# Block 6 of the first expert layer moves from direct products to seven block products per pair of tiles, in a three-layer fp32 kernel on one core

## The chip, the cores and the metric

The kernel runs on one NeuronCore of one Trainium2 chip. The metric is the device time of one execution in microseconds (us), smaller is better. Engines are named as in the profile: PE is TensorE (PEld its weight loads), DVE is VectorE, ACT is ScalarE, POOL is GpSimd, SP is SyncE, whose queue (SPq) issues all the transfers here.

## The reference

```
q_s = softmax(q, over head_dim);  k_s = softmax(k, over seq)          # 8 x 8 x 576 x 64
attn = q_s @ (k_s^T @ v)           ->  x: 4608 tokens x 512
h = x @ w_in (512 x 2048);  g = elu(h);  x = g @ w_out                # layer 1
h = x @ w2_in;  g = P(h) / Q(h), a cubic over a quadratic in |h|;  out = g @ w2_out   # layer 2
```

All of it is float32. The inputs are scaled by 8, so full precision matters.

## The kernel before, in words

**Precision.** A float32 matrix product is made of three fp32r products: each operand is split into a high and a low part (`copy_hi`, `sub_lo`), and high·high, high·low and low·high are summed in PSUM.

**Blocks and tiles.** The 4608 tokens are nine blocks of 512 (`NB` = 9, `j` = 0 to 8), the 2048 hidden columns sixteen tiles of 128 (`KF` = 16, `f`). A step is one tile of one block, in the order of the list `tiles`.

**Direct form** (layer 1, blocks 0 to 6): `plan_in` (L1157) makes a tile of h by 12 products of 128x512 into a PSUM bank (L1169 to L1171); ACT and DVE form elu and its two parts (`plan_elu`, L1372); `plan_out` (L1191) adds 12 products of 128x512 into the accumulators (L1208). A pair of tiles is 24 products in and 24 out.

**Seven-product form** (layer 1, blocks 7 and 8, and all of layer 2): `plan_group` (L1471) makes two tiles as a 2x2 block product by seven products of sums (m1 to m7 at L1559 on). Each is six matmuls of 128x256 (L1508), 42 in all, into a pair of PSUM banks; between them ACT copies two quarters (u1, u5, L1517) and DVE adds two (d2, d1, L1522), and m6, m7 and m4 wait for those. The out half is the same 24 matmuls of 128x512 (L1601 in layer 1, L1741 in layer 2). The sums of weights (`w1f` for layer 1, `wf` for layer 2) and of x (`x0`, `x1`) are formed beforehand by DVE, POOL and ACT, saved to DRAM and loaded again: every group loads 1.75 MB of weight sums (`plan_ring`, L1421, loads named `ring`), and every block seven forms of x (`plan_xf`, loads named `xf`).

`J0` is the first block in this form; there are `N1` = (9 - J0) * 8 groups in layer 1. The eight weight sums of layer 1 are formed once (`plan_w1f`), whatever J0 is.

**Attention.** Pairs of heads: load k and v, softmax of k over the sequence, the key-value product (`kv_pair`, L774, issued by `plan_unit`, L1063), the softmax of q (`plan_q`), and x itself (`x_mm` in `plan_x`, L887). `at_step` and `x_step` say at which step a pair's key-value product and x are wanted; the tables `EARLIER` and `X_STEP` override them. In layer 1's groups x is computed in a pair of banks between two groups (`in_pair`, `between`), and the forms of x go straight to their tiles (`plan_here`); for block J0 alone they go through DRAM (`x0_d`).

**The order.** A planner (`Plan`) sets it when the program is built: every operation has engines, a cost, what it waits for and a rank; `run` picks the next one by the earliest start and then the rank, and the engines get their instructions in that order. `NUDGE` adds to the rank of single operations by number, `W2FROM` and `W2STEP` say at which steps layer 2's weights are converted (32 loads `st`, `plan_w2`). Each engine, and the SP queue, then runs its list in order.

```
for p in range(HALF if J0 < NB else 0):
    plan_w1f(p, W1FROM + W1STEP * p)
...
for j in range(J0, NB):
    plan_xf(0, j)
    for p in range(HALF):
        plan_group(0, j, p)
```

Of the kernel before, what the change touches and what calls it, by code (L numbers as in the profile page):

```python
# [25 lines left out]
J0 = 7  # L26
# [21 lines left out]
W2FROM, W2STEP = 44, 2.4  # L48
# [27 lines left out]
NUDGE = {3: 12, 20: -40.7, 27: 71.1, 37: 14.9, 45: 23.6, 47: -20.6, 57: -10.7, 58: -13.2, 60: 28.4, 68: -37, 69: -15.2, 70: -43.5, 94: -35.9, 95: 27, 99: 8.1, 104: 3, 109: -5.8, 112: 4.2, 121: 19.8, 130: 52.7, 131: -5.5, 135: 33.7, 158: 18.9, 168: 27.2, 209: 8.6, 211: 28.6, 213: 1.2, 221: 4.8, 223: -3.4, 226: 66.8, 235: 75.5, 250: 40.1, 278: 66.9, 304: -20.3, 313: 0.7, 315: -48.8, 650: 18.7, 656: 6.8, 694: 35.3, 908: 6.8, 918: 28.6, 1619: -25.7, 1624: 17.2, 1756: 11.5, 1822: 3.2, 1839: -3.7, 1884: 15.7, 1890: 5.2, 1892: 18.7, 1909: -1.9, 1953: -8.3, 1978: 17.9, 2019: -6.8, 2029: -11.1, 2205: 18.9, 2433: -5.3, 2911: 59.4, 2946: 10, 2964: 31.4, 2994: 9.7, 3002: -4.3}  # L76
# [210 lines left out]
def linear_attention_elu_rational(  # L287
# [295 lines left out]
    def plan_w2(f, which, rank, after):  # L583
# [23 lines left out]
        b["op"] = op(SP, load, after, rank - 1, take=[kinds], extra=6.0, move=MB)  # L607
        o, x = plan_f32(b["op"], lambda: b["st"], high, DM, rank, [], front)
        if which:
# [1326 lines left out]
```

## Time and profile before

| | |
|---|---|
| median of 3 runs | 1531.74 us (1531.17 to 1534.08) |
| the profiled execution: time, span | 1529.98 us, 1528.2 us |
| PE busy | 1517.4 us, 99% of the span |
| PEld, DVE, ACT, POOL busy | 89%, 77%, 69%, 37% |
| granted TensorE clock | 1.0 (2.4 GHz) in all slices |
| DMA | 358.90 MB, 235 GB/s over the span |

The span runs from the first to the last instruction; the time is 1.78 us longer. The busy share of PE counts a matmul to its modelled end, so two matmuls overlap in it: what one costs is read from the distance of starts. In the slices PE stands at 9 tenths or more in all but the first and the last.

### The profile page before, as it was taken

Reading aid. Unit: us, or ns where it says so; the run is one execution under the profiler, and the core shown is the slowest. Engines: PE = TensorE matmul, PEld = TensorE weight load, DVE = VectorE, ACT = ScalarE, POOL = GpSimd, SP = SyncE. Lnnn points to the kernel's source line nnn. Section 1 sums busy time; section 2 is a strip of 40 time slices with the busy share of each in tenths; the row PEclk is TensorE's granted clock in tenths of the full one; section 3 lists DMA queues with packets and bytes.
Section 4 is the critical chain, followed back from the end, with each engine's and each line's share of the span. In section 5 each row is a group of like instructions: output and inputs, shape, how many; then the busy total and the mean of one; then the engine's idle time right before and its main releaser. Section 6 shows DMA issues by size and latency. Waiting matters only on the chain.

```text
span 1528.2 us, 26062 instructions
## 1 busy us (share of the span) xinstructions
PE 1517.4 (99%) x9916; PEld 1361.5 (89%) x9916; DVE 1171.7 (77%) x1710; ACT 1061.8 (69%) x1630; POOL 572.9 (37%) x355
## 2 busy tenths in 40 slices
PE   8999999999999999999999999999999999999998
PEld 6888888888888888898999999999999999999998
DVE  8998899776869888577656787777777777777776
ACT  7877666665757666576557777777777777777775
POOL 3103344221313222033125775444444444444442
PEclk9999999999999999999999999999999999999999
DMA  9622775444544555787999987766767675757561
GB/s 372 260 84 74 239 269 198 167 174 149 195 153 160 183 197 221 257 291 288 335 370 387 371 286 259 255 255 227 270 212 274 218 280 207 290 206 275 207 228 49
DMA packets 99997, 358.90 MB, mean 235 GB/s; under 512 B 9760, under 2 KB 22048, under 8 KB 85536
## 3 DMA queue, kind: packets, MB, share of 16 engines
q1 hardware_dynamic: 99872, 357.23, 64.5%
q8 instruction: 78, 1.28, 0.3%
q14 instruction: 47, 0.39, 0.1%
HBM read 271.21 MB, written 85.98 MB: 234 GB/s over the span
## 4 chain that ended last, share of the span: by engine, by line
PE 96%; DVE 2%; DMA 1%; issue 0%; ACT 0%; POOL 0%; SPq 0%; DVEq 0%; POOLq 0%
PE pair L1508 26%; PE acc L1741 24%; PE acc L1208 19%; PE ps L1169 6%; PE ps L1171 6%; PE ps L1170 6%; PE acc L1601 5%; PE ps L784 1%; PE ps L916 1%; DMA st<-in_moe_w_in_dram 0%; DMA e<-in_q_dram 0%; PE ps L796 0%; DVE mx L845 0%; DVE bits L459 0%; DVE mx L815 0%
## 5 line engine op out<-in xcount | busy, mean ns | idle before, releaser
L1508 PEld LDWEIGHTS pair<-xf,ring 128*128 128x128 f32 x3696 | 453.4, 192 | 16.6 <-ACT pair L1517 1.3
L1508 PE MATMUL pair<-xf,ring 128*128 128x256 f32 x3696 | 456.1, 275 | 1.2 <-ACT pair L1517 0.9
L1741 PE MATMUL acc<-w_out,g 128*128 128x512 f32 x1728 | 407.4, 379 | 0.0
L1741 PEld LDWEIGHTS acc<-w_out,g 128*128 128x128 f32 x1728 | 311.1, 190 | 35.1
L1208 PE MATMUL acc<-gs,w_out 128*128 128x512 f32 x1344 | 310.5, 380 | 0.0
L1643 POOL TENSOR_TENSOR s<-s,a 128x1024 f32<-128x1024 f32 x72 | 170.6, 2369 | 338.8 <-ACT s L1635 316.7
L1208 PEld LDWEIGHTS acc<-gs,w_out 128*128 128x128 f32 x1344 | 252.5, 189 | 38.1 <-issue 1.0
L1169 PE MATMUL ps<-xp,w_in 128*128 128x512 f32 x448 | 171.6, 383 | 0.0
L1522 DVE TENSOR_TENSOR pair<-pair,u 128x256 f32<-128x256 f32 x176 | 75.9, 431 | 122.9 <-PE pair L1508 122.7
L1170 PE MATMUL ps<-xp,w_in 128*128 128x512 f32 x448 | 169.8, 379 | 0.0
L1171 PE MATMUL ps<-xp,w_in 128*128 128x512 f32 x448 | 169.8, 379 | 0.0
L438 POOL TENSOR_TENSOR g<-p,g 128x1024 fp32r<-128x1024 f32 x70 | 166.9, 2384 | 7.7 <-POOL s L1643 0.4
L1630 ACT ACTIVATE a<-pair,b_sb 128x1024 f32<-128x1024 f32 (+1 forms) x73 | 80.4, 1103 | 125.6 <-PE pair L1508 125.6
L1660 DVE TENSOR_TENSOR p<-p,pair 128x1024 f32<-128x1024 f32 (+1 forms) x73 | 88.1, 1206 | 71.9 <-ACT s L1635 67.3
L435 ACT ACTIVATE gs<-halves 128x512 fp32r<-128x512 f32 x112 | 70.5, 630 | 73.7 <-DVE halves L1396 33.6
L1390 ACT ACTIVATE halves<-ps 128x512 f32<-128x512 f32 x112 | 66.4, 593 | 58.0 <-PE ps L1171 56.8
L1396 DVE SCALAR_TENSOR_TENSOR halves<-halves,ps 128x512 f32<-128x512 f32 x112 | 75.7, 678 | 34.9 <-ACT halves L1393 34.5
L1169 PEld LDWEIGHTS ps<-xp,w_in 128*128 128x128 f32 x448 | 84.6, 189 | 15.1 <-issue 2.4
L1656 DVE SCALAR_TENSOR_TENSOR a<-s,a 128x1024 f32<-128x1024 f32 (+1 forms) x73 | 95.7, 1312 | 2.4
L1171 PEld LDWEIGHTS ps<-xp,w_in 128*128 128x128 f32 x448 | 84.7, 189 | 12.0
L1667 DVE SCALAR_TENSOR_TENSOR p<-p,a_sb,a 128x1024 f32<-128x1024 f32 (+1 forms) x74 | 93.5, 1265 | 2.5
L1170 PEld LDWEIGHTS ps<-xp,w_in 128*128 128x128 f32 x448 | 84.7, 189 | 11.5
(178 smaller groups left out, 2258.9 us busy)
## 6 DMA issues: line engine op xcount, KB each, us to landing
ring<-wf SPq DMA_DIRECT2D x72, 1024.0 KB, 5.1
ring<-wf SPq DMA_DIRECT2D x72, 768.0 KB, 7.1
x<-fo SPq DMA_DIRECT2D x60, 512.0 KB, 3.2
xf<-x SPq DMA_DIRECT2D x30, 1024.0 KB, 7.8
ring<-w1f SPq DMA_DIRECT2D x16, 1024.0 KB, 5.4
wf<-fo SPq DMA_DIRECT2D x24, 512.0 KB, 3.1
ring<-w1f SPq DMA_DIRECT2D x16, 768.0 KB, 7.2
out_dram<-e SPq DMA_DIRECT2D x36, 256.0 KB, 2.2
```

Of the source, the lines that this page charges most:

```text
L438: engine[e].tensor_tensor(out=lo, in0=src, in1=hi.bitcast(F32), op=ALU.subtract)
L1169: nc.tensor.matmul(o, w[:, 0, kk, :], two(x[:, 0]), start=(kk == 0), stop=False)
L1170: nc.tensor.matmul(o, w[:, 0, kk, :], two(x[:, 1]), start=False, stop=False)
L1171: nc.tensor.matmul(o, w[:, 1, kk, :], two(x[:, 0]), start=False, stop=(kk == KD - 1))
L1208: nc.tensor.matmul(turned(o), lhsT, two(rhs), start=(f == f0 and n == 0), stop=(f == f1 and n == 2))
L1508: apart(nc.tensor.matmul(o, lhsT, two(rhs), start=start and n == 0, stop=n == 5, skip_group_check=True), "PE", where[region])
L1630: nc.scalar.activation(out=b["a"][:, c], in_=h(), func=AF.Abs, scale=b_sb[:, 0:1])
L1643: engine[e].tensor_tensor(out=b["s"][:, c], in0=b["s"][:, c], in1=b["a"][:, c], op=ALU.add)
L1656: nc.vector.scalar_tensor_tensor(out=b["a"][:, c], in0=b["s"][:, c], scalar=-2.0, in1=b["a"][:, c], op0=ALU.add, op1=ALU.mult)
L1660: nc.vector.tensor_tensor(out=b["p"][:, c], in0=b["p"][:, c], in1=h(), op=ALU.mult)
L1667: nc.vector.scalar_tensor_tensor(out=b["p"][:, c], in0=b["p"][:, c], scalar=a_sb[:, 0:1], in1=b["a"][:, c], op0=ALU.add, op1=ALU.mult)
L1741: nc.tensor.matmul(turned(o), b["g"][:, gl, c], two(wo[:, wl_]), start=p == 0 and q == 0 and n == 0, stop=p == KF // 2 - 1 and q == 1 and ...
```

## The change

Block 6 of layer 1 goes from `plan_elu` tiles to eight `plan_group` groups (`J0` 7 to 6), so layer 1 has 24 groups, not 16. The key-value products and x of blocks 6 and 7 get earlier steps, and layer 2's weights are converted from step 36 on, not 44. Key-value products of blocks 6 and 7 now go to the upper half of their two banks, and one matmul of 128x256 per bank, on any weights, writes the lower half behind them (two per unit, four units). The planner's costs of two transfers of layer 2's weights change, and the table of nudges from number 950 on.

```diff
-J0 = 7
+J0 = 6
...
-EARLIER = {..., (6, 0): 81.5, (6, 1): 86.5, (7, 0): 93, (7, 1): 97.5}
-X_STEP = {(7, 0): 99, (7, 1): 103}
+EARLIER = {..., (6, 0): 77, (6, 1): 81.5, (7, 0): 88, (7, 1): 91}
+X_STEP = {(6, 0): 84, (6, 1): 88}
...
-W2FROM, W2STEP = 44, 2.4
+W2FROM, W2STEP = 36, 2.4
...
+        assert i not in opened
...
-        b["op"] = op(SP, load, after, rank - 1, take=[kinds], extra=6.0, move=MB)
+        b["op"] = op(SP, load, after, rank - 1, take=[kinds], extra=6.0, move=0.5 * MB)
...
-            stored["wo", f] = o = op(SP, save, [o], rank, free=[("fo", own)], extra=SAVE, move=MB)
+            stored["wo", f] = o = op(SP, save, [o], rank, free=[("fo", own)], extra=SAVE, move=0.5 * SAVE_MB)
...
+            covered = n // NP >= J0 and n not in in_pair
             for m, t in zip(ab, banks):
-                m["pk"] = t[:, 0:D + 1]
+                m["pk"] = t[:, TB // 2:TB // 2 + D + 1] if covered else t[:, 0:D + 1]
...
-            if n in in_pair:
-                any_w = slot[KF - 1, 1][:, 0]
-                nc.tensor.matmul(pair[:, TB:TB + TB // 2], any_w[:, 0:P], any_w[:, 0:TB // 2], start=False, stop=True,
-                                 skip_group_check=True)
+            any_w = slot[KF - 1, 1][:, 0]
+            for part in [pair[:, TB:TB + TB // 2]] if n in in_pair else [t[:, 0:TB // 2] for t in banks if covered]:
+                nc.tensor.matmul(part, any_w[:, 0:P], any_w[:, 0:TB // 2], start=False, stop=True, skip_group_check=True)
...
         if n in in_pair:
             between(u, in_pair[n])
+        elif 0 in first_of:
+            behind(first_of[0], u)
```

Three places of the order are used below. Lines of the change stand one to three higher than those of before.

The first is PE where the first group of layer 1 starts. `xp,w_in` are in-products of the last direct tiles, `gs,w_out` their out-products, `xf,ring` the block products (six of one m each), `g,w_out` the first group's out-products. Before, m1, m5 and m6 stand in one row of 18, then m7 between in-products; and further on 36 in one row:

```order
L1171 MATMUL ps<-xp,w_in 128x512
L1508 MATMUL pair<-xf,ring 128x256 x18
L1169 MATMUL ps<-xp,w_in 128x512
L1170 MATMUL ps<-xp,w_in 128x512
L1171 MATMUL ps<-xp,w_in 128x512
L1169 MATMUL ps<-xp,w_in 128x512
L1170 MATMUL ps<-xp,w_in 128x512
L1171 MATMUL ps<-xp,w_in 128x512
L1508 MATMUL pair<-xf,ring 128x256 x6
```

The change has m1 alone, six rows of one, ahead of the last 24 in-products; the last of these is the first row here:

```order
L1174 MATMUL ps<-xp,w_in 128x512
L1211 MATMUL acc<-gs,w_out 128x512 x12
L1511 MATMUL pair<-xf,ring 128x256 x12
L1211 MATMUL acc<-gs,w_out 128x512 x15
L1511 MATMUL pair<-xf,ring 128x256 x6
L1211 MATMUL acc<-gs,w_out 128x512 x9
L1511 MATMUL pair<-xf,ring 128x256 x36
L1211 MATMUL acc<-gs,w_out 128x512 x3
L1511 MATMUL pair<-xf,ring 128x256 x24
L1211 MATMUL acc<-gs,w_out 128x512 x9
L1604 MATMUL acc<-g,w_out 128x512 x12
```

So m6 no longer follows m1 and m5 of an otherwise empty row, and the row of 36 (m2, m3, m4 of the first group, m1, m5, m6 of the second) has 9 out-products before it, where it had 39.

The second is PE behind the last key-value unit ahead of the groups (`vb,kt` and `vt,kt`; the two last rows of 36 products). Before:

```order
L784 MATMUL ps<-vb,kt 64x65 x2
L784 MATMUL ps<-vt,kt 64x65 x2
L1169 MATMUL ps<-xp,w_in 128x512
L1170 MATMUL ps<-xp,w_in 128x512
L1171 MATMUL ps<-xp,w_in 128x512
```

and in the change, with the two covering matmuls at L790:

```order
L786 MATMUL ps<-vb,kt 64x65 x2
L786 MATMUL ps<-vt,kt 64x65 x2
L790 MATMUL ps<-w_out 128x256 x2
L1211 MATMUL acc<-gs,w_out 128x512 x12
L1172 MATMUL ps<-xp,w_in 128x512
```

The unit is as long as before and has two matmuls of 128x256 behind it.

The third is DVE from the second add of the first group (d1) to the first add of the second (d2). `st` are layer 2's weights, `qt` and `mx` the softmax of q, `fo` forms to be saved, `halves` and `gs` the elu of direct tiles. Before, the eleven last rows up to d2:

```order
L1396 SCALAR_TENSOR_TENSOR halves<-halves,ps 128x512
L438 TENSOR_TENSOR fo<-wa,fo 128x256
L438 TENSOR_TENSOR fo<-st,fo 128x512
L438 TENSOR_TENSOR gs<-halves,gs 128x512
L1396 SCALAR_TENSOR_TENSOR halves<-halves,ps 128x512
L438 TENSOR_TENSOR gs<-halves,gs 128x512 x2
L815 TENSOR_REDUCE mx<-qt 128x16
L459 TENSOR_SCALAR st<-st 128x512
L463 TENSOR_SCALAR st<-st 128x512
L754 COPY mx<-mx 32x16 x4
L1522 TENSOR_TENSOR pair<-pair,u 128x256
```

and in the change all that stands between the two adds:

```order
L1525 TENSOR_TENSOR pair<-pair,u 128x256
L460 TENSOR_SCALAR st<-st 128x512
L464 TENSOR_SCALAR st<-st 128x512
L816 TENSOR_REDUCE mx<-qt 128x16
L472 SCALAR_TENSOR_TENSOR st<-st 128x512
L439 TENSOR_TENSOR fo<-t,fo 128x2x256
L755 COPY mx<-mx 32x16 x4
L1525 TENSOR_TENSOR pair<-pair,u 128x256
```

The elu of the direct tiles is done ahead of d1 now, and the piece between the adds is short.

## Rows read from the trace of the kernel before

**Rows 1.** Windows of the whole span: busy us (and instructions) per engine, granted clock, DMA.
```profile
core 0: us, PE busy (x) PEld busy (x) DVE busy (x) ACT busy (x) POOL busy (x), PEclk, DMA share, GB/s
0.00:60.00 60.00, 54.66 (x450) 42.73 (x451) 52.74 (x98) 47.21 (x80) 20.35 (x22) 1.00 0.82 312
60.00:620.00 560.00, 560.00 (x3505) 480.19 (x3505) 466.00 (x879) 377.96 (x767) 147.35 (x136) 1.00 0.52 180
620.00:760.00 140.00, 138.43 (x879) 125.33 (x878) 97.39 (x166) 87.33 (x147) 34.19 (x33) 1.00 0.85 300
760.00:1520.00 760.00, 760.00 (x5069) 709.81 (x5068) 555.19 (x570) 547.08 (x634) 370.97 (x164) 1.00 0.70 258
1520.00:1528.20 8.20, 4.34 (x21) 3.45 (x19) 0.42 (x1) 2.17 (x4) 0.00 (x0) 1.00 0.33 128
```

**Rows 2.** Timeline of PE, direct tiles: start, us, what, then count.
```profile
611.13 5.34 PE L1208 MATMUL acc<-gs,w_out 128*128 128x512 f32 x24
616.31 0.38 PE L1169 MATMUL ps<-xp,w_in 128*128 128x512 f32 x1
...
624.08 2.10 PE L1208 MATMUL acc<-gs,w_out 128*128 128x512 f32 x9
```

**Rows 3.** The chain that ended last, a group of layer 1: start, us, what.
```profile
749.68 2.68 PE pair L1508 x24
752.36 1.95 PE acc L1601 x9
```

**Rows 4.** Timeline of PE: the rows with idle time before them, 620 to 760 us.
```profile
633.81 0.94 PE L1508 MATMUL pair<-xf,ring 128*128 128x256 f32 x6 [0.46 <-ACT pair L1517]
...
652.82 0.94 PE L1508 MATMUL pair<-xf,ring 128*128 128x256 f32 x6 [0.46 <-ACT pair L1517]
...
690.41 0.94 PE L1508 MATMUL pair<-xf,ring 128*128 128x256 f32 x6 [0.26 <-DVE pair L1522]
...
743.74 1.35 PE L1601 MATMUL acc<-g,w_out 128*128 128x512 f32 x5 [0.39 <-DVE g L438]
```

**Rows 5.** The chain, the piece ahead of the last of these.
```profile
734.22 7.17 DMA st<-in_moe_w_in_dram
...
741.41 0.76 DVE st L459
742.16 1.53 DVE g L438
```

**Rows 6.** Windows: layer 1's sixteen groups, and the fullest 20 us of DMA.
```profile
631.00:789.00 158.00, 156.43 (x1027) 142.89 (x1026) 104.59 (x172) 94.79 (x156) 37.93 (x35) 1.00 0.87 313
800.00:820.00 20.00, 20.00 (x135) 18.69 (x134) 10.84 (x13) 13.12 (x16) 2.38 (x1) 1.00 1.00 386
```

**Rows 7.** Groups by line, DVE: busy us, mean ns of one, idle before.
```profile
L1396 DVE SCALAR_TENSOR_TENSOR halves<-halves,ps 128x512 f32<-128x512 f32 x112 | 75.7, 678 | 34.9 <-ACT halves L1393 34.5 <-PE acc L1208 0.3
L438 DVE TENSOR_TENSOR gs<-halves,gs 128x512 fp32r<-128x512 f32 x81 | 59.5, 734 | 28.2 <-ACT gs L435 27.7
L1575 DVE SCALAR_TENSOR_TENSOR halves<-halves,pair 128x1024 f32<-128x1024 f32 x16 | 19.5, 1221 | 15.0 <-ACT halves L1572 15.0
L438 DVE TENSOR_TENSOR g<-halves,g 128x1024 fp32r<-128x1024 f32 x16 | 24.4, 1528 | 0.6 <-ACT g L435 0.6
L1522 DVE TENSOR_TENSOR pair<-pair,u 128x256 f32<-128x256 f32 x176 | 75.9, 431 | 122.9 <-PE pair L1508 122.7
```

**Rows 8.** The same view: what stands between two adds of groups in the change's order.
```profile
L459 DVE TENSOR_SCALAR st<-st 128x512 int16<-128x512 int16 x32 | 26.7, 833 | 3.6 <-DMA st<-in_moe_w_out_dram 2.1 <-DMA st<-in_moe_w_in_dram 1.5
L463 DVE TENSOR_SCALAR st<-st 128x512 int32<-128x512 int32 x32 | 19.9, 622 | 0.0
L815 DVE TENSOR_REDUCE mx<-qt 128x16 f32<-128x512 f32 (+1 forms) x18 | 12.1, 675 | 0.7 <-DMA qt<-in_q_dram 0.7
L471 DVE SCALAR_TENSOR_TENSOR st<-st 128x512 int32<-128x512 int32 x16 | 13.5, 846 | 4.2 <-ACT st L467 3.6
L438 DVE TENSOR_TENSOR fo<-t,fo 128x512 fp32r<-128x512 f32 x63 | 48.3, 768 | 9.0 <-ACT fo L435 6.2 <-DMA w_out<-wo 2.6
L754 DVE COPY mx<-mx 32x16 f32<-32x16 f32 x96 | 22.8, 238 | 1.6
```

More of the change, by code (lines that the diff above doesn't have):

```diff
@@ L29 @@
 AT_PAIR = 7.26
-EARLIER = {(3, 0): 33.5, (3, 1): 38.5, (4, 0): 49.5, (4, 1): 54.5, (5, 0): 65.5, (5, 1): 70.5, (6, 0): 81.5, (6, 1): 86.5, (7, 0): 93, (7, 1): 97.5}
-X_STEP = {(7, 0): 99, (7, 1): 103}
+EARLIER = {(3, 0): 33.5, (3, 1): 38.5, (4, 0): 49.5, (4, 1): 54.5, (5, 0): 65.5, (5, 1): 70.5, (6, 0): 77, (6, 1): 81.5, (7, 0): 88, (7, 1): 91}
+X_STEP = {(6, 0): 84, (6, 1): 88}
 UNIT_AT = 2, 6
@@ L74 @@
 FLOOR = -32768.0 + 16 * 896
-NUDGE = {3: 12, 20: -40.7, 27: 71.1, 37: 14.9, 45: 23.6, 47: -20.6, 57: -10.7, 58: -13.2, 60: 28.4, 68: -37, 69: -15.2, 70: -43.5, 94: -35.9, 95: 27, 99: 8.1, 104: 3, 109: -5.8, 112: 4.2, 121: 19.8, 130: 52.7, 131: -5.5, 135: 33.7, 158: 18.9, 168: 27.2, 209: 8.6, 211: 28.6, 213: 1.2, 221: 4.8, 223: -3.4, 226: 66.8, 235: 75.5, 250: 40.1, 278: 66.9, 304: -20.3, 313: 0.7, 315: -48.8, 650: 18.7, 656: 6.8, 694: 35.3, 908: 6.8, 918: 28.6, 1619: -25.7, 1624: 17.2, 1756: 11.5, 1822: 3.2, 1839: -3.7, 1884: 15.7, 1890: 5.2, 1892: 18.7, 1909: -1.9, 1953: -8.3, 1978: 17.9, 2019: -6.8, 2029: -11.1, 2205: 18.9, 2433: -5.3, 2911: 59.4, 2946: 10, 2964: 31.4, 2994: 9.7, 3002: -4.3}
+NUDGE = {3: 12, 20: -40.7, 27: 71.1, 37: 14.9, 45: 23.6, 47: -20.6, 57: -10.7, 58: -13.2, 60: 28.4, 68: -37, 69: -15.2, 70: -43.5, 94: -35.9, 95: 27, 99: 8.1, 104: 3, 109: -5.8, 112: 4.2, 121: 19.8, 130: 52.7, 131: -5.5, 135: 33.7, 158: 18.9, 168: 27.2, 209: 8.6, 211: 28.6, 213: 1.2, 221: 4.8, 223: -3.4, 226: 66.8, 235: 75.5, 250: 40.1, 278: 66.9, 304: -20.3, 313: 0.7, 315: -48.8, 650: 18.7, 656: 6.8, 694: 35.3, 908: 6.8, 918: 28.6, 1359: -21.6, 1382: 3.7, 1385: -12, 1510: -8.6, 1513: -11, 1542: 2.6, 1634: -29.3, 1636: -8.9, 1645: 13.4, 1649: 22.1, 1653: -6.6, 1697: 6.4, 2118: 13.2, 2283: -13.1, 3014: 4.6, 3022: -10.4, 3025: -22.4, 3043: 21.6, 3057: 11.7, 3107: 2.9}
 class Plan:
```

## The prediction

> **What bounds the kernel now.** I read the windows of the whole span first [rows 1]. PE is busy for all of 60 to 620 us and all of 760 to 1520 us: not a microsecond is idle there, while DVE stands at 83% and 73%, ACT at 67% and 72%. PE's idle time is 5.34 us in the first 60 us, 3.86 us at the end and 1.57 us between 620 and 760 us, 10.8 us in all. So the time is PE's own work, and a change is worth what it takes from PE's list plus what it does to the waits around 620 to 760 us, where layer 1 goes over from the direct form to the groups. The granted clock is 1.0 in every window, its upper level of 2.4 GHz, so clock is no term.
>
> What one matmul costs must not be read from the mean durations, because neighbours overlap; I read it from distances of starts. In the direct form 24 out-products start at 611.13 us and the next matmul at 616.31 us, and the 36 in-products from there reach to 624.08 us [rows 2]: 5.18 us / 24 and 7.77 us / 36, both **215.8 ns** for 128x512. In a group of layer 1, 24 block products take 2.68 us [rows 3]: **111.7 ns** for 128x256. The 9 out-products behind them take 1.95 us, 216 ns again, so the out half costs the same in both forms.
>
> The four idle pieces are in the timeline [rows 4]. Two of 0.46 us stand where m6 follows m1 and m5 without other work and ACT's copy of m1 isn't done. Two are accidents of a full DVE queue: 0.26 us when an add came late, and 0.39 us when DVE's low part of g came late. The chain tells the last one [rows 5]: a load of layer 2's weights took 7.17 us, the conversion of it (floor) stood first in DVE's queue and waited, and the low part of g, which the out-products need, was behind it.
>
> **The change, part by part.**
>
> *Products.* Eight pairs of tiles lose 24 in-products of 128x512 each, 192 in all: 192 x 215.8 ns = 41.43 us. They get 42 products of 128x256 each, 336: 336 x 111.7 ns = 37.53 us. The 192 out-products only change their line. Net **-3.90 us**, all of it on the path, since PE is the path. It is 9.4% of the in half and not an eighth, because 256 columns cost 111.7 ns, more than half of 215.8.
>
> The Trainium skill speaks of that price, in "TensorE: Matmul & The Clock Gate", section "Back-to-back issue gap": a warm matmul by itself follows the last after its columns at 2.4 GHz plus about 2.5 ns, an estimate of 215.8 ns for 512 columns and 109.2 ns for 256. The first agrees with the trace to the digit; the second is 2.5 ns below what the groups show, and by it the sum below would be -3.9 us instead of -3.0. The measured one is taken, since it comes from the very instructions that are added.
>
> *Covering matmuls.* Four units of key-value products get two 128x256 each, eight in all. No such matmul stands in the trace of before; the nearest row has the same shape, 111.7 ns [rows 3], so **+0.89 us**. From below: nothing, if they hide in the change from the short key-value products to full ones; from above 215.8 ns each, 1.73 us. I take the nearest row. They wait for nothing new: their weights are in place long before.
>
> *The start of the groups.* In the new order m1 stands alone ahead of 24 in-products, so u1 is done long before m6: the first 0.46 us wait goes, **-0.46 us**. The second stays, since m6 of the second group still follows m1 and m5 in the row of 36. What is late next would be d1 and d2 on DVE. Between them stand two conversions, a maximum, a join, a form and four copies [rows 8]: 833 + 622 + 675 + 846 + 768 + 4 x 238 = 4.70 us, with d1's 0.43 us [rows 7] 5.1 us. On PE 9 out-products and 36 block products cover that: 1.94 + 4.02 = 5.96 us. It fits, with 0.8 us to spare, if the floor's load and the load of q have landed.
>
> *More groups.* The accidents, 0.65 us over 16 groups, will come again over 24. By the number of groups that is 0.98 us. By the number of x units that stand between two groups, four instead of two (block 7's are among them now), it is 1.30 us. Between the two I take **+0.49 us** more than before; the ends are +0.33 and +0.65 us.
>
> *DVE, ACT and POOL, at nothing.* A group costs DVE one elu of 1221 ns, one low part of 1528 ns and two adds of 431 ns in place of two of 678 and two of 734 ns [rows 7]: 3.61 against 2.82 us, 6.3 us for eight groups. PE covers it: in the sixteen groups of before DVE was busy for 66% of the time and ACT for 60% [rows 6]. The forms of block 7's x now go straight to their tiles and those of block 6 take the way through DRAM that block 7's had; the work is the same. If the cover were gone, each group could lose up to its 0.8 us.
>
> *Queues.* SP issues 16 more ring loads, 14.7 MB, and the x loads of block 6 instead of block 7's. Counting the new order by size, the 22 stretches from the third ring load to the last of layer 1 hold 68.9 MB, 3.13 MB each; in the order of before 14 such stretches hold 44.6 MB, 3.18 MB each. So DMA has as much to do per group as before, when it moved 313 GB/s there; it has moved 386 GB/s without an idle moment of PE [rows 6]. The fullest new group has 4.2 MB, 10.9 us at that rate against a group's 24 x 215.8 + 42 x 111.7 ns = 9.87 us of PE, and the next ones are lighter. Key-value products, x and the weights of layer 2 move ahead by 4 to 8 steps of 5.2 us; what they are moved past on DVE is a stretch where it is 83% busy and PE never waits [rows 1]. Cost: nothing.
>
> **Sum.** -3.90 + 0.89 - 0.46 + 0.49 = -2.98 us. Against the profiled execution that is 1529.98 - 3.0 = 1527.0 us; its time is 1.76 us below the median of the runs shown, so the median goes from 1531.74 to **1528.7 us**. That is 0.195%, and 0.2% (3.06 us) is about what a measurement of this kernel can tell from no change: the forecast sits on that line.
>
> **The rivals.**
>
> *DVE eats part of it.* Place: d2 between m6 and m7 of each group. For it: DVE gets 6.3 us more, just where it also has attention and layer 2's weights to do. Against it: over the whole kernel DVE stood idle for 122.7 us ahead of its 176 adds, waiting for PE [rows 7]. If each of the 24 groups loses 0.1 us, 2.4 us where the sum has 1.14, the sum is -1.7 us; with 0.2 us each it is +0.7 us, 1532.4 us.
>
> *Slower: the floor in front of the adds.* The piece at 743 us again and again: a load of layer 2's weights comes late, the floor halts DVE's queue, and d1, d2 or the low part of g wait behind it. In the new SP order nine such loads stand in the groups, seven before. For it: it happened, and the new order has a floor right behind d1 of the first group. Against it: seven such loads cost 0.39 us together. It decides for "slower" when each of the nine costs over 0.67 us (6.04 us together); at 0.8 us each the sum is -3.0 + 7.2 = +4.2 us, 1535.9 us.
>
> *Cheaper products.* If 256 columns cost half of 512, 107.9 ns, the products give -41.43 + 36.25 us and the covering ones +0.86 us: with the waits -4.3 us, 1527.4 us. The block products of layer 1 say otherwise [rows 3]. By the Trainium skill's gap for 256 columns (same page and section), an estimate, the time would be 1527.8 us.
>
> That the change doesn't do what it says is excluded by its order: it holds 4032 block products where there were 3696, and 1152 direct in-products where there were 1344.
>
> **How the numbers follow.** The sum as it stands, from -4.0 to -2.0 us: 0.72, of which a little over half lies beyond 3.06 us, because the covering matmuls may hide in part: 0.40 faster, 0.32 same. Part eaten: 0.10, same. Cheaper products: 0.06, faster. Slower: 0.12. Together faster 0.46, same 0.42, slower 0.12. The sum's own range is 1527.7 to 1529.7 us. The whole range goes from 1526.9 us (cheaper products, and half a microsecond for the spread of the runs, 1531.17 to 1534.08) to 1533.7 us, 2 us above before, which leaves out most of the slower case.
>
> **What would show it.** In the profile of the changed kernel: 24 block products in 2.68 us, from about 545 us on (16 tiles of 5.2 us before the 632 us of now); two covering matmuls taking 0.2 us behind each of four key-value units; one ACT wait of 0.46 us at the start of the groups, not two; PE's idle time between 60 and 1520 us at about 1.6 us. I am wrong if that idle time is over 3 us (then DVE or a load is the cause, and the rows before the waits name it), or if block products stand further apart than 111.7 ns in block 6.

## The result, and the profile after

The changed kernel takes **1543.44 us** (median of 4 runs, 1542.6 to 1544.91), the kernel before 1531.45 us beside it (4 runs): a ratio of **1.0078**, 95% interval 1.006 to 1.0096. Forecast were 1528.7 us, with 1533.7 us as the upper end. So the change is slower by 12 us, outside the range.

The profiled execution has a span of 1543.1 us, 14.9 us more than before. Its windows, five stretches of it (columns as in [rows 1]):

```profile
200.00:260.00 60.00, 57.74 (x413) 47.41 (x412) 53.76 (x111) 44.06 (x112) 27.22 (x25) 1.00 0.70 241
420.00:440.00 20.00, 17.26 (x135) 13.57 (x133) 15.13 (x34) 13.53 (x30) 8.16 (x7) 0.91 0.44 155
500.00:560.00 60.00, 58.40 (x422) 48.72 (x421) 49.25 (x99) 43.31 (x101) 13.86 (x12) 1.00 0.72 258
560.00:620.00 60.00, 55.39 (x332) 48.89 (x331) 39.56 (x78) 34.32 (x61) 14.80 (x13) 0.97 0.89 306
620.00:760.00 140.00, 139.43 (x945) 126.92 (x944) 107.06 (x181) 88.34 (x153) 55.09 (x45) 1.00 0.84 294
```

Between 60 and 620 us, where PE was never idle before [rows 1], it now is for 11.2 us; in 620 to 760 us, where all its waits were, 0.57 us are left. In two stretches the granted clock is below 1.00. The first group starts at 561.4 us, not at 545: most of the loss lies ahead of it, in the direct form. Whom PE waits for, by line (us in total, times, longest):

```profile
PE acc L1211 <- DVE gs L439: 4.3, 5, 2.6
PE pair L1511 <- DMA xf<-x: 2.2, 2, 2.0
PE pair L1511 <- ACT pair L1520: 2.0, 2, 1.5
```

What was forecast of PE's own work stands in the trace. 24 block products take 2.68 us here too (the chain: start, us, what), as in [rows 3]:

```profile
715.38 2.68 PE pair L1511 x24
```

And the covering matmuls, in the timeline of PE behind a key-value unit that began at 552.07 us:

```profile
553.28 0.50 PE L790 MATMUL ps<-w_out 128*128 128x256 f32 x2
553.62 2.75 PE L1211 MATMUL acc<-gs,w_out 128*128 128x512 f32 x12
```

Two of them take 0.34 us to the next start, and so at all four units. But not all of this is new: before, the first matmul of 128x512 behind a key-value unit (here the unit at 571.76 us) takes 0.32 us to the next start, 0.10 us more than its 0.2158 us, and behind the covering matmuls the 128x512 takes 0.216 us again.

```profile
572.97 0.48 PE L1169 MATMUL ps<-xp,w_in 128*128 128x512 f32 x1
573.29 0.38 PE L1170 MATMUL ps<-xp,w_in 128*128 128x512 f32 x1
```

So a pair of covering matmuls adds 0.34 - 0.10 = 0.24 us to PE's list, 0.96 us at the four units, where 0.89 us was taken.

For the rest I need one measure that holds idle time and a slow clock alike. **Lost time** of PE is the distance of two starts less what stands between them at the prices of [rows 2, 3]: 215.8 ns for 128x512, 111.7 ns for 128x256 (and 1.21 us for the 72 matmuls of a key-value unit). An example is the pair of rows of PE at 429 us below: from the start of 11 out-products to the next start are 4.26 us, 11 x 0.2158 = 2.37 us, so 1.89 us are lost there though PE isn't idle. Summed from 100 to 900 us, for every kernel of this study (one profile each; the ratio is to the kernel before on the same chip). A row of the timeline is counted where it begins, so what is lost close to 560 us can stand one column too far left, by about 1 us in e11 and e13; e1's longest wait, which ends at 630 us, is counted where it lies.

| kernel | 220-260 | 420-440 | 500-560 | 560-620 | 620-760 | 100-900 | span less that | ratio |
|---|---|---|---|---|---|---|---|---|
| before | 0.5 | 0.4 | 0.6 | 0.6 | 4.3 | 9.2 | 1519.0 | 1 |
| changed | 4.4 | 5.4 | 3.2 | 8.1 | 3.3 | 27.4 | 1515.7 | 1.0078 |
| e1 | 0.8 | 0.4 | 5.1 | 9.2 | 19.8 | 38.0 | 1515.7 | 1.0118 |
| e2 (J0 = 7) | 4.5 | 5.3 | 3.7 | 1.5 | 20.9 | 39.6 | 1518.3 | 1.0168 |
| e3 | 4.5 | 5.2 | 4.6 | 10.7 | 22.8 | 51.0 | 1515.8 | 1.0259 |
| e4 (J0 = 7) | 0.6 | 0.4 | 0.6 | 0.6 | 16.8 | 22.6 | 1517.8 | 1.0068 |
| e5 (J0 = 7) | 0.8 | 0.3 | 0.4 | 0.4 | 7.6 | 15.5 | 1518.5 | 1.0025 |
| e8 | 3.7 | 5.4 | 3.1 | 8.4 | 27.5 | 51.1 | 1515.0 | 1.0218 |
| e9 (J0 = 7) | 1.4 | 0.4 | 1.0 | 0.6 | 12.6 | 19.4 | 1518.2 | 1.0054 |
| e10 | 3.6 | 5.1 | 4.3 | 5.6 | 2.2 | 23.9 | 1514.9 | 1.0054 |
| e11 | 0.7 | 0.4 | 3.5 | 2.5 | 6.1 | 17.4 | 1515.2 | 1.0017 |
| e12 | 1.5 | 0.4 | 2.5 | 11.0 | 4.2 | 24.9 | 1515.2 | 1.0061 |
| e13 | 0.6 | 0.4 | 2.2 | 5.3 | 4.4 | 16.1 | 1514.9 | 1.0007 |
| e14 | 0.6 | 0.4 | 2.2 | 2.7 | 4.9 | 14.0 | 1515.4 | 1.0009 |
| e15 | 0.6 | 0.4 | 1.4 | 3.0 | 8.3 | 18.4 | 1515.0 | 1.0011 |
| e16 | 0.6 | 0.4 | 3.5 | 6.0 | 2.4 | 16.3 | 1514.9 | 1.0002 |

Two things are to be seen. The last column but one is what PE itself needs: 1514.9 to 1515.8 us in the eleven kernels with the new products, 1517.8 to 1519.0 us in the five without. Between the means, 1515.2 and 1518.4 us, lie 3.1 us, with a spread of about 1 us in either set: the products and their covers give what was forecast of them (3.90 - 0.89 = 3.0 us). And the changed kernel loses 27.4 us where before lost 9.2: 18.2 us more, of which 3.9, 5.0, 2.6 and 7.5 us stand in the first four stretches.

**The two largest waits, read from the trace.** At 429 us the out-products wait for the low part of gs. The chain of the changed kernel ahead of it (start, us, what):

```profile
422.78 0.22 ACT mx L753
...
423.47 0.93 ACT st L468
424.39 0.47 ACT halves L1393
...
424.88 0.64 ACT halves L1396
...
425.55 0.45 DVE halves L1399
...
426.15 0.70 DVE qT L836
426.86 0.62 DVE fo L439
427.48 1.68 DVE gs L439
```

and PE and POOL in the timeline:

```profile
429.21 4.33 PE L1211 MATMUL acc<-gs,w_out 128*128 128x512 f32 x11 [2.63 <-DVE gs L439]
433.47 0.28 PE L786 MATMUL ps<-vb,kt 64*64 64x65 f32 x2
```

```profile
427.16 1.45 POOL L439 TENSOR_TENSOR gs<-halves,gs 128x512 fp32r<-128x512 f32 x1 [0.23 <-ACT gs L436]
428.57 2.37 POOL L644 TENSOR_TENSOR t<-wa 128x256 f32<-128x256 f32 x2
```

No transfer is late here. ACT works without a pause, but small copies of the softmax (mx) and the scaling of layer 2's weights (st) stand ahead of the two elu steps (halves), and on DVE a transpose and a low part stand ahead of gs. This gs itself is long: 1.75 us, where the median of DVE's 74 is 0.69 us. POOL worked beside it all the time. In this trace the 62 that had no two-operand operation (TENSOR_TENSOR) of POOL beside them took 0.73 us at most, and all six above 0.9 us had one. So about 1 us of the wait, an estimate from 1.75 - 0.69, goes with what stood beside gs on POOL, and only the rest with what stood in front of it. (e2 below has the same gs of 1.75 us in this place, e13 none over 0.9 us behind 160 us.) PE stood 2.63 us, and then the 11 products took 387 ns each. The windows say why:

```profile
430.00:432.00 2.00, 2.00 (x6) 1.57 (x5) 1.97 (x5) 1.38 (x5) 0.94 (x1) 0.50 0.40 168
...
574.00:576.00 2.00, 2.00 (x7) 1.55 (x6) 1.85 (x5) 0.35 (x1) 0.00 (x0) 0.50 1.02 349
```

The granted clock is 0.50, its lower level of 1.2 GHz, behind this wait and behind the other large one, at 572 us. That one is a load of x forms (the timeline of PE, then of SP):

```profile
571.99 2.05 PE L1511 MATMUL pair<-xf,ring 128*128 128x256 f32 x12 [2.00 <-DMA xf<-x]
```

```profile
562.30 0.53 SPq L1455 DMA_DIRECT2D xf<-x  x1
```

and this load by itself, with who waited for it:

```profile
who waited for it (us, times):
  PE pair L1511: 2.0, 1
...
DMA to landing us min/median/max: 9.6/9.6/9.6
```

The load was issued at 562.30 us, 0.9 us after the groups had begun, and landed 9.6 us later. The last x forms of block 6 come later still: their save runs from 563.91 us for 9.22 us and the load behind it is issued at 573.14 us, but PE waits only 0.16 us for that one (at 581.25 us). The loads of x forms take 9.6 us from issue to landing between 560 and 620 us; at the start of before's groups (620 to 680 us) 6.5 us. The issues of both kernels (KB each, median us to landing), the changed one's first:

```profile
xf<-x SPq DMA_DIRECT2D x3, 1024.0 KB, 9.6
```

```profile
xf<-x SPq DMA_DIRECT2D x3, 1024.0 KB, 6.5
```

The longest wait behind these two, 1.50 us at 609.12 us for a copy of ACT (L1520), begins on ACT with two form copies whose buffer isn't saved yet:

```profile
602.56 0.42 ACT L436 ACTIVATE fo<-e 128x256 fp32r<-128x256 f32 x1 [3.82 <-DMA wo<-fo]
604.44 0.63 ACT L436 ACTIVATE fo<-t 128x512 fp32r<-128x512 f32 x1 [1.46 <-DMA wf<-fo]
```

Behind them ACT goes on without a pause, up to the copy that PE waits for.

### The profile page after: what moved, and what is told of

Same layout as the page of the kernel before. It is cut to its first block, busy times and chain, and to the rows that moved or that the text cites. A ratio compares the mean times of both kernels' runs of the same rounds, so it can differ in the third digit from the quotient of the medians.

```text
span 1543.1 us, 26425 instructions
## 1 busy us (share of the span) xinstructions
PE 1522.6 (99%) x10068; PEld 1365.8 (89%) x10068; DVE 1166.6 (76%) x1680; ACT 1074.3 (70%) x1671; POOL 584.3 (38%) x356
## 4 chain that ended last, share of the span: by engine, by line
PE 84%; DMA 8%; DVE 4%; ACT 2%; issue 2%; POOL 0%; SPq 0%; ACTq 0%; POOLq 0%; DVEq 0%
PE pair L1511 27%; PE acc L1744 24%; PE acc L1211 12%; PE acc L1604 6%; PE ps L1172 4%; PE ps L1174 4%; PE ps L1173 4%; DMA wf<-fo 2%; DMA x<-fo 2%; DMA kt<-in_k_dram 1%; DVE fo L439 1%; PE ps L786 1%; DMA bits<-in_moe_w_out_dram 1%; DMA st<-in_moe_w_in_dram 1%; PE ps L917 1%
## 5 line engine op out<-in xcount | busy, mean ns | idle before, releaser
L1511 PEld LDWEIGHTS pair<-xf,ring 128*128 128x128 f32 x4032 | 495.0, 192 | 23.0 <-ACT pair L1520 2.5
L1511 PE MATMUL pair<-xf,ring 128*128 128x256 f32 x4032 | 498.6, 275 | 4.8 <-DMA xf<-x 2.2
L1211 PE MATMUL acc<-gs,w_out 128*128 128x512 f32 x1152 | 271.6, 384 | 5.7 <-DVE gs L439 4.3
L1211 PEld LDWEIGHTS acc<-gs,w_out 128*128 128x128 f32 x1152 | 217.8, 191 | 42.4 <-DVE gs L439 6.4
L1172 PE MATMUL ps<-xp,w_in 128*128 128x512 f32 x384 | 147.3, 384 | 0.3 <-DVE halves L1399 0.3
L1173 PE MATMUL ps<-xp,w_in 128*128 128x512 f32 x384 | 145.5, 379 | 0.0
L1174 PE MATMUL ps<-xp,w_in 128*128 128x512 f32 x384 | 145.5, 379 | 0.0
L1604 PE MATMUL acc<-g,w_out 128*128 128x512 f32 x576 | 137.4, 380 | 0.4 <-DVE g L439 0.4
L1604 PEld LDWEIGHTS acc<-g,w_out 128*128 128x128 f32 x576 | 103.3, 190 | 13.9 <-ACT mx L753 0.8
L436 ACT ACTIVATE gs<-halves 128x512 fp32r<-128x512 f32 x96 | 60.6, 631 | 55.2 <-PE acc L1211 25.9
L1666 DVE SCALAR_TENSOR_TENSOR p<-p,a_sb,pair 128x1024 f32<-128x1024 f32 (+1 forms) x73 | 92.3, 1266 | 2.5
L1655 DVE SCALAR_TENSOR_TENSOR s<-s,a 128x1024 f32<-128x1024 f32 (+1 forms) x73 | 88.7, 1216 | 3.2 <-POOL g L439 3.0
```

The costliest lines, as they stand in the source:

```text
L1172: nc.tensor.matmul(o, w[:, 0, kk, :], two(x[:, 0]), start=(kk == 0), stop=False)
L1173: nc.tensor.matmul(o, w[:, 0, kk, :], two(x[:, 1]), start=False, stop=False)
L1174: nc.tensor.matmul(o, w[:, 1, kk, :], two(x[:, 0]), start=False, stop=(kk == KD - 1))
L1211: nc.tensor.matmul(turned(o), lhsT, two(rhs), start=(f == f0 and n == 0), stop=(f == f1 and n == 2))
L1511: apart(nc.tensor.matmul(o, lhsT, two(rhs), start=start and n == 0, stop=n == 5, skip_group_check=True), "PE", where[region])
L1604: nc.tensor.matmul(turned(accs[0, j, i]), w[:, wl_, c], two(b["g"][gl][:, cols]), start=p == 0 and q == 0 and n == 0, stop=p == HALF - 1 a ...
```

## The experiments

Four theories. **A**: the work that was moved ahead (layer 2's weights, attention) is too much for DVE, ACT and SP where it now stands. **B**: the first group's x comes too late. **C**: the place of single operations in the queues decides, that is how the planner's table of nudges fits the order, not the amount of work. **D**, in e10: transfers are crowded at the start of the groups.

**e1: layer 2's weights from step 44 again.**

```diff
-W2FROM, W2STEP = 36, 2.4
+W2FROM, W2STEP = 44, 2.4
```

> The changed kernel with the conversion of layer 2's weights from step 44 on again, not 36. Theory A, too much work moved ahead (the conversions now share DVE, ACT and SP with attention in the direct form, and PE waits for gs and elu): the 3.9 us lost at 220 to 260 us come back, and part of the 5.0 us at 420 to 440 us; time 1535 to 1539 us. Theory B, the first group's x comes too late (save of the forms, then load, PE idle 2.0 us at 572 us): nothing comes back ahead of 500 us that counts, 1541 to 1544 us. Theory C, the order alone (the nudges fit one order, and any shift of the list spoils it): the losses move to other places, 1541 to 1547 us.

1551.16 us, ratio 1.0118 (1.0081 to 1.0154). That is slower than any of the three had it. The 3.9 and 5.0 us come back where A said (all but 0.3 us, by the table), and 17.6 us more are lost behind 560 us. The windows of e1:

```profile
200.00:260.00 60.00, 60.00 (x430) 50.44 (x428) 57.82 (x119) 42.07 (x105) 31.28 (x29) 1.00 0.63 223
...
420.00:440.00 20.00, 20.00 (x170) 16.72 (x169) 18.02 (x40) 15.16 (x35) 4.53 (x4) 1.00 0.58 202
...
620.00:760.00 140.00, 127.40 (x824) 115.11 (x823) 94.73 (x161) 77.69 (x133) 39.70 (x36) 0.95 0.78 272
```

The largest new wait is 8.14 us, for one copy of 0.58 us. ACT's timeline, and PE's row behind it:

```profile
626.81 0.63 ACT L436 ACTIVATE fo<-t 128x512 fp32r<-128x512 f32 x1 [5.63 <-DMA x<-fo]
627.35 1.04 ACT L436 ACTIVATE g<-halves 128x1024 fp32r<-128x1024 f32 x1
628.29 0.66 ACT L468 ACTIVATE st<-st 128x512 f32<-128x512 f32 x1
628.86 0.61 ACT L436 ACTIVATE fo<-e 128x512 fp32r<-128x512 f32 x1
629.38 0.58 ACT L947 ACTIVATE e<-pair 128x512 f32<-128x512 f32 x1
```

```profile
630.00 2.93 PE L1511 MATMUL pair<-xf,ring 128*128 128x256 f32 x12 [8.14 <-ACT e L947]
```

ACT stands in front of a form copy whose buffer (fo) isn't saved yet; the copy e, which empties the pair of banks for the next group's m1, is four places behind it. The Trainium skill says in "TensorE: Matmul & The Clock Gate", section "Architectural detail: the array is 16× 32×32, not 1× 128×128", that the queues of ACT and DVE are strict FIFO; the row at 626.81 agrees, with 5.63 us in which nothing behind it ran. So step 44 gives back what step 36 cost, and another accident takes more: A's place and C's result.

**e3: without the changed kernel's own nudges** (its entries from number 1359 on taken out: 20 of them, not 22).

> The changed kernel with only those entries of the table of nudges that it shares with the kernel before; its 22 own ones are gone. Theories A and B: they shift single operations by fractions of a step, and the losses at 220 to 260, 425 and 570 us stay; 1542 to 1546 us. Theory C, the order alone: the time changes by 3 us or more either way, and other places than those three lose.

1572.06 us, ratio 1.0259 (1.0243 to 1.0275). 28.6 us slower than the changed kernel, all of it behind 500 us: 13.3 us of waits of the kind that e1 showed. What A and B name stayed: 4.5 and 5.2 us at 220 to 260 and 420 to 440 us, and PE waits 3.7 us for x.

**e4: before without its own nudges** (its entries from number 1619 on).

> The kernel before with only those entries of the table of nudges that it shares with the changed one. Theories A and B: what it does ahead of 620 us is the same work at the same steps, and PE goes on without a wait there; 1531 to 1534 us. Theory C, the order alone: the kernel before is fast because its table was fitted to it; without the fitted part it loses 5 us or more, 1536 to 1546 us, in the direct form as the changed kernel does.

1542.05 us, ratio 1.0068 (1.0053 to 1.0083), in C's range, but not where C put it: nothing is lost in the direct form, all of it behind 620 us, 8.2 us in one wait for e. With neither's own nudges the two kernels are 30 us apart, not 12: the change makes the order harder, and its table hides a part of that.

**e5: before with the sooner attention of blocks 6 and 7.**

```diff
-EARLIER = {..., (6, 0): 81.5, (6, 1): 86.5, (7, 0): 93, (7, 1): 97.5}
+EARLIER = {..., (6, 0): 77, (6, 1): 81.5, (7, 0): 88, (7, 1): 91}
```

> The kernel before with the key-value products of blocks 6 and 7 at the steps of the changed kernel (77, 81.5, 88, 91 for 81.5, 86.5, 93, 97.5), all else as it was. Theory A, too much work moved ahead: PE loses 3 to 8 us between 400 and 560 us, where the attention of these blocks now meets the weights of layer 2; 1534 to 1540 us. Theory B, the first group's x: here block 7's forms are late and its kv is sooner, nothing waits; 1531 to 1533 us. Theory C, the order alone: any shift loses, 1534 to 1546 us, at places that have nothing to do with blocks 6 and 7.

1536.3 us, ratio 1.0025 (1.0015 to 1.0035). A's time, but not its place: 400 to 560 us loses nothing, 3.3 us more are lost at 620 to 760 us, and 2.6 us between 760 and 900 us (2.9 against 0.3). That is C's sort, at a small price.

**e2: before with step 36.**

```diff
-W2FROM, W2STEP = 44, 2.4
+W2FROM, W2STEP = 36, 2.4
```

> The kernel before with the conversion of layer 2's weights from step 36 on, as in the changed kernel, not 44; all else as it was. Theory A, work moved ahead overfills the queues in front of a direct form where PE was never kept waiting: PE loses 7 to 10 us at 220 to 260 and 420 to 440 us, the two places where the changed kernel lost 8.9 us and where it lost nothing with step 44; what the conversions leave free behind 620 us gives back at most the 4 us that before loses there; 1536 to 1542 us. Theory C, the order alone: the table of nudges is before's own, whose fit is broken; 5 us or more are lost behind 600 us as well, 1541 to 1552 us. If step 36 were free, as predicted: 1530 to 1533 us.

1559.46 us, ratio 1.0168 (1.0151 to 1.0185), slower than any theory had it. The windows show the two losses of the changed kernel again, in a kernel that has none of its products:

```profile
200.00:260.00 60.00, 57.64 (x406) 47.57 (x399) 52.47 (x110) 42.79 (x109) 27.24 (x25) 1.00 0.71 239
420.00:440.00 20.00, 16.97 (x136) 13.36 (x139) 14.81 (x33) 13.37 (x31) 8.15 (x7) 0.91 0.39 159
```

So the step is their cause: 4.0 and 4.9 us here, 3.9 and 5.0 us there. Of the rest, 21.5 us, the most is one wait and what follows it at a lower clock (0.95 over 620 to 760 us):

```profile
PE pair L1508 <- ACT e L946: 13.3, 1, 13.3
```

**e8 and e9: the tables of nudges exchanged** (the changed kernel with before's, before with the changed kernel's).

> The changed kernel with the whole table of nudges of the kernel before in place of its own; a third draw of the order for the same work at the same steps. Theory C, the order alone decides by chance: the time lies anywhere from 1540 to 1575 us, with the same 8.9 us at 220 to 260 and 420 to 440 us (those places did not move without nudges) and other losses behind 500 us. Theory A alone: 1541 to 1547 us.

> The kernel before with the whole table of nudges of the changed kernel in place of its own. Theory C: as without nudges (1542 us) or worse, 1536 to 1555 us, all of it behind 600 us. Theory A alone: 1531 to 1535 us. If the work of the changed kernel is heavier on the queues at the start of the groups by itself, three draws of before (own 1532, none 1542, this) lie lower than three draws of the changed kernel (own 1543, none 1572, and before's).

e8 1566.62 us (two runs), ratio 1.0218 (1.0197 to 1.024); e9 1541.99 us, ratio 1.0054 (1.0038 to 1.007). Three orders of before lose 9.2, 22.6 and 19.4 us, three of the changed kernel 27.4, 51.0 and 51.1 us. So for tables of the same three kinds the changed kernel loses 18 to 32 us more, and 9 us of that are step 36's. That speaks against C alone, but three orders are few, and e11 to e16 find better ones.

**e10: the changed kernel with less to load, in its own order.**

```diff
+    loaded = lambda n, part: 4 - part if n < 2 or n >= N1 else 2 - part
...
-                nc.sync.dma_start(out=b[part].bitcast(F32), in_=wd[p][:, lo:hi])
+                nc.sync.dma_start(out=b[part].bitcast(F32)[:, 0:loaded(n, part)], in_=wd[p][:, lo:lo + loaded(n, part)])
...
-                        lhsT = w[part][:, k, ...]
+                        lhsT = w[part][:, k % loaded(n_group, part), ...]
```

> The changed kernel in its own order, but in layer 1 the loads of the weight ring bring, from the third group on, 3 of 7 block forms instead of 7 (2 for 4 and 1 for 3), and the block products read those three in place of all seven; the sums of layer 1's last blocks are so not the reference's. Every engine has the same instructions in the same order; 22 groups x 4 x 256 KB = 23 MB less to move between 560 and 800 us. Theory D, the transfers are crowded at the start of the groups (DMA 88% busy from 560 to 620 us; loads of x forms take 9.6 us there, 6.5 us before), so that ACT and DVE stand behind transfers and PE behind them: of the 9 us that PE loses from 560 to 740 us more than it did before, 5 to 8 come back; 1535 to 1538 us. Theory C, the place of each operation in the queues alone: 1 us or less comes back, 1541 to 1544 us.

1541.14 us, ratio 1.0054 (1.0039 to 1.007). Windows of e10:

```profile
560.00:620.00 60.00, 55.77 (x353) 50.33 (x353) 43.42 (x84) 35.36 (x65) 17.88 (x14) 1.00 0.74 250
620.00:760.00 140.00, 140.00 (x948) 127.80 (x948) 104.06 (x177) 88.98 (x150) 53.32 (x44) 1.00 0.62 201
```

DMA falls from 0.89 to 0.74 and from 0.84 to 0.62, and 3.6 us come back where D wanted 5 to 8 and C 1 at most (8.1 + 3.3 to 5.6 + 2.2 us). But the first lighter load is issued only at 580.83 us. Ahead of that nothing is lighter (DMA 0.90 at 560 to 575 us, 0.83 in the changed kernel), and PE waits 3.3 us for x, at 570.65 and 579.86 us: whether crowding makes these loads late, e10 doesn't test. Its granted clock stays at 1.00 in both windows, so the 1.75 us that the changed kernel lost at the lower clock behind 572 us are not lost here. Behind the two waits for x PE's idle time falls from 3.0 to 0.9 us, and the wait of 1.50 us behind ACT's form copies is gone. So crowding costs about 2 us there; D as the cause of the whole isn't shown.

**e11 and e12: other nudges.** Both tables were chosen by trying entries in the planner with transfers counted longer; the times are the chip's. e12 has only 69 more entries, e11 other steps too:

```diff
-EARLIER = {..., (6, 0): 77, (6, 1): 81.5, (7, 0): 88, (7, 1): 91}
-X_STEP = {(6, 0): 84, (6, 1): 88}
+EARLIER = {..., (6, 0): 76, (6, 1): 79.5, (7, 0): 86, (7, 1): 89.5}
+X_STEP = {(6, 0): 86, (6, 1): 88}
...
-W2FROM, W2STEP = 36, 2.4
+W2FROM, W2STEP = 38, 2.6
...
-CROWD = 500.0
+CROWD = 350.0
...
-extra=6.0, move=0.5 * MB)
+extra=6.0, move=MB)
...
-extra=SAVE, move=0.5 * SAVE_MB)
+extra=SAVE, move=MB)
```

> The changed kernel with the same 336 block products and covering matmuls, but another order around them: layer 2's weights from step 38 on, every 2.6 steps (36, 2.4); key-value products of blocks 6 and 7 at 76, 79.5, 86, 89.5; block 6's x at 86 and 88; the costs of layer 2's transfers as the kernel before had them (a whole MB, not half); and a table of nudges chosen anew so that no operation on ACT or DVE stands in front of PE behind a transfer, with transfers counted at the lengths that the trace shows. Theory C, only the order is at fault: PE loses no more than before (9 us between 100 and 900 us), and what the products give remains; 1524 to 1531 us. Theory A or D, the groups cannot start 70 us sooner without PE waiting, whatever the order: 1536 to 1545 us, with the waits at 500 to 620 us still there.

> The changed kernel with its own steps, costs and products, and 69 more entries in the table of nudges, chosen in the same way as in the run beside it; nothing else differs. Theory C: most of the 15 us come back with the steps as they are, also part of the 8.9 us at 220 to 260 and 420 to 440 us; 1528 to 1535 us. Theory A, step 36 and the sooner attention cost this by the amount of work in one place: 1538 to 1545 us, and 220 to 260 and 420 to 440 us lose what they lost.

e11 1534.14 us, ratio 1.0017 (1.0006 to 1.0028), 3 us above C's range and 2 us below that of A and D; it loses 17.4 us, not 9. e12 1541.0 us, ratio 1.0061 (1.0041 to 1.0082): a time that A forecast, but not at A's places. e12's windows:

```profile
200.00:260.00 60.00, 59.77 (x438) 49.70 (x431) 56.16 (x113) 42.91 (x108) 29.75 (x27) 1.00 0.70 240
420.00:440.00 20.00, 20.00 (x170) 16.72 (x169) 17.46 (x36) 14.38 (x29) 6.23 (x5) 1.00 0.54 202
...
560.00:620.00 60.00, 54.54 (x327) 48.39 (x325) 41.44 (x81) 32.06 (x59) 15.12 (x14) 0.94 0.84 298
```

With step 36 kept, the same work in these stretches now costs 1.5 and 0.4 us, not 4.4 and 5.4. DVE is even busier than in the changed kernel (56.16 against 53.76 us, 17.46 against 15.13 us). Part of it has moved: PE idles 1.4 us between 260 and 420 us, where it doesn't idle in before and in the changed kernel. e13 below settles this. e12 still loses 11.0 us at the start of the groups, with a wait of 1.9 us for x.

**e13 and e14: x sooner, and e11's order once more.** e13 is the changed kernel with block 6's x four tiles sooner, the costs of e11, `CROWD` at 200 and 96 new nudges; e14 is e11 with its nudges chosen again.

```diff
-X_STEP = {(6, 0): 84, (6, 1): 88}
+X_STEP = {(6, 0): 80, (6, 1): 84}
```

> The changed kernel with all its steps (layer 2's weights from step 36, attention of blocks 6 and 7 where it put it) but one: block 6's x forms at steps 80 and 84, not 84 and 88, four tiles sooner; costs of layer 2's transfers as before, transfers counted from 200 us on, and the nudges chosen anew with these. Theory B, the first group's x comes too late, as one cause beside the order: the loads of x are there when the groups start, PE's wait for them (2.2 us, and 1.75 us at half clock behind it, in the changed kernel; 2.0 us in the run with the nudges alone) goes below 0.5 us, and 560 to 620 us loses 3 us or less; 1529 to 1533 us. If the x steps don't matter: the wait for x stays at 1 us or more, 1534 to 1540 us.

> The run before last but one (layer 2's weights from step 38, x at 86 and 88; 1534.1 us) with its nudges chosen once more, against several lengths of the transfers instead of one. Theory C: the 17.4 us that PE still lost there between 100 and 900 us come down to 12 to 15 us, 1529 to 1533 us. If the groups' sooner start costs by itself, whatever the order: 1533 to 1537 us, with 15 us or more lost and 6 us or more of it between 540 and 760 us.

e13 1532.93 us, ratio 1.0007 (0.9997 to 1.0016); e14 1532.08 us, ratio 1.0009 (1.0 to 1.0019). Neither can be told from before, and e14 is where C had it. e13 keeps step 36 and the sooner attention, and its windows settle A:

```profile
200.00:260.00 60.00, 60.00 (x436) 50.58 (x429) 57.17 (x112) 42.71 (x106) 30.72 (x28) 1.00 0.69 240
420.00:440.00 20.00, 20.00 (x170) 16.71 (x169) 15.05 (x34) 11.70 (x25) 5.66 (x5) 1.00 0.69 229
```

PE has no idle time between 60 and 545 us there, as in before. So it isn't the amount of work that costs but which operations stand in front of, and beside, the ones that PE waits for. In e13 the wait for x is 0.9 us, not below 0.5, and 560 to 620 us loses 5.3 us: B isn't shown by it. e11 and e14 both have the first of the two x units later than the changed kernel (86, 88); e11 waits 1.4 us for x, e14 shows no such wait. So the step of x alone doesn't decide whether it is late. e14's windows and its longest wait in layer 1:

```profile
560.00:620.00 60.00, 58.82 (x388) 53.02 (x387) 48.01 (x91) 36.41 (x62) 25.96 (x24) 1.00 0.84 291
620.00:760.00 140.00, 138.06 (x923) 125.35 (x922) 102.89 (x171) 88.16 (x146) 39.02 (x34) 1.00 0.86 301
```

```profile
PE pair L1511 <- DVE pair L1525: 2.0, 3, 0.8
```

**e15 and e16: is the rest order as well?** e15 is e14 with its nudges chosen a third time; e16 has layer 2's weights from step 40 (every 2.6), attention at 78, 81.5, 88 and 89.5, x where the change put it, `CROWD` at 200, e11's costs and nudges of its own.

> The second refit (layer 2's weights from step 38, 1532.1 us) with its nudges chosen a third time, against transfers and operations of several lengths. Theory C, all of the rest is order too: PE loses 12 us or less between 100 and 900 us, 1527 to 1530.5 us, below before. If the groups' start and their greater number keep what the products give: 13 us or more lost, most of it between 540 and 760 us, 1531 to 1534 us.

> The changed kernel with block 6's x where the change put it (84, 88), layer 2's weights from step 40 on, every 2.6 steps, attention of blocks 6 and 7 at 78, 81.5, 88, 89.5, the costs of transfers as before, and nudges chosen as in the run beside it: another order far from that one. Theory C: 1527 to 1531 us, and the x at its own steps costs nothing once the order around it fits. If the x comes too late at these steps whatever the order: a wait of 1 us or more for x at the first groups, 1532 to 1536 us.

e15 1533.86 us, ratio 1.0011 (0.9999 to 1.0023); e16 1532.86 us, ratio 1.0002 (0.9991 to 1.0013). Neither beats before, and they lose 18.4 and 16.3 us. Both miss what C forecast and come out where the other expectation was: e15 loses over 13 us, most of it behind 540 us, and e16, with x at the change's own steps, waits 1.2 us for x at 551 us. Losses change their place from order to order (e15 8.3 us at 620 to 760 us, e16 6.0 us at 560 to 620 us), but behind 500 us no order of the new products lost less than 9.8 us, and before loses 5.5. Whether a better order exists is open: the ones tried were found with the planner's costs, which don't know what the chip does to each.

## Why the prediction was wrong

*Products, covers, and the waits that were summed: right.* PE's own list became 3.1 us shorter; 3.0 us was forecast for products and covers, and the covers add 0.96 us where 0.89 us was taken. One of the two waits of 0.46 us is gone, the other stands at 585.33 us. The accidents, for which 0.65 + 0.49 = 1.14 us was forecast, are 1.07 us: in the groups PE waits so long for adds and low parts of DVE.

*The step that failed* is the last one under "Queues": "Key-value products, x and the weights of layer 2 move ahead by 4 to 8 steps of 5.2 us; what they are moved past on DVE is a stretch where it is 83% busy and PE never waits [rows 1]. Cost: nothing." Where this work went, PE loses 19 us more (3.9 + 5.0 + 2.6 + 7.5). 8.9 us of them are shown to be step 36's, in two kernels (e1, e2). The other 10.1 us stand at the start of the groups and just ahead of them, and no run takes them apart. The loads of x took 9.6 us there, which the step, counting MB per stretch, put at nothing too. That PE never waits between 60 and 620 us I read as slack of the stretch; it was a property of one order of the queues. e2 shows that one number, 36 for 44, takes it away in the kernel before, and e13 that the same work with step 36 can stand there without a wait of PE. A busy share doesn't hold this: DVE is less busy in the stretches of the changed kernel where PE waits than in those of e12 where it doesn't.

*The table of nudges* is named among the changes and was not priced. e3 and e4 show what it is worth: 28.6 us in the changed kernel, 9.7 us before (1542.05 - 1532.36).

*"The granted clock is 1.0 in every window, so clock is no term"* was true of before alone. Two waits of 2.63 and 2.00 us brought 1.89 and 1.75 us more at the lower level.

*The slower rival* had the right sort of event, an operation that stands in a queue in order behind a transfer, and the wrong place: floors ahead of adds in the groups, nine times over 0.67 us. Adds and low parts of the groups cost 1.07 us in all, 0.65 us before. In the changed kernel it was elu and low parts behind other work and beside POOL's, loads of x that took 9.6 us, and once ACT's copy between two products (L1520) behind form copies that wait for their buffer; in orders that fit less it is the copy e that stands behind such a form copy. *DVE eats part of it* also looked only at the groups.

*What would show it*: "wrong if that idle time is over 3 us (then DVE or a load is the cause)" came true, with 11.8 us and with DVE's gs and the loads of x as the first two rows of the waits. The groups were to begin at 545 us and began at 561.4. The 545 was a slip of its own: 16 tiles of 5.2 us are 83.2 us, and 632 - 83.2 = 548.8 us; in e13 and e14, which lose little ahead of the groups, they begin at 549.1 and 548.7 us. With the 11.7 us lost ahead of them in the changed kernel (15.9 us between 100 and 560 us against 4.2) that makes 560.5 us.

*What is shown and what isn't.* Shown: the products give 3 us; step 36 in the change's order costs 8.9 us in two places (e1, e2) and need not (e13); the order as a whole is worth over 10 us, since four kernels with the same products and other orders (e13 to e16) can't be told from before. Not shown: what the 10.1 us behind 500 us in the changed kernel are made of one by one, how much of the loads' 9.6 us is crowding, and why the best of the other orders still lose 5 us more than before. More groups (24, not 16) and less direct form to hide other work in is a likely reason that no run tests.

## What to carry to other kernels

Where an order is fitted to one set of steps, a change that moves steps must be judged with its order, not by adding up work: PE without a wait in a stretch is a result of the order, not room for more. Before a step of work is put at nothing, look at what stands directly in front of each operation that PE waits for on ACT and DVE, which of these wait for a buffer that a save has to free, and what POOL does beside them. And measure a change against one or two other orders of both kernels: 3 us of work can't be seen through 10 to 30 us of order.

## What the runs showed of the hardware

PE's granted clock fell to 0.50 behind single waits of 2.63 us (at 429 us) and 2.00 us (at 572 us) in the changed kernel, each time after PE had already gone on; the stretches 432 to 434 us and 576 to 578 us show 0.76 and 0.92 again. What followed at the lower level cost 1.89 and 1.75 us, nearly as much as the waits.

A change of shape has a price that the first matmul behind it pays: behind the 64x65 products of a key-value unit a 128x512 takes 0.32 us to the next start, not 0.216 us (all twelve units of before); a covering 128x256 takes 0.22 us, the second of the pair 0.12 us, and the 128x512 behind them 0.216 us (all four covered units of the changed kernel).

DVE's low part of gs, with two operands of 128x512, took 0.73 us at most in the changed kernel when POOL ran no two-operand operation beside it (62 of 74), and 1.75 us where POOL did so for the whole time. The six above 0.9 us all had POOL beside them.
